# Agent attention with a mixture-of-experts tail: the list scheduler's prices for transfers and its table of urgencies

## The chip, the cores and the metric

The kernel runs on one core of a Trainium2 chip. The core has five engines with an instruction queue each: TensorE (PE in the profile, its weight loads PEld), VectorE (DVE), ScalarE (ACT), GpSimd (POOL) and SyncE (SP), which issues nearly all transfers. The metric is the device time of one execution in microseconds, as the median of several runs.

## The reference

Four batches of 12608 tokens with 128 channels, 49 agents per batch. What is computed:

```python
def _attn_ref(q, k, v, agents):
    a2k = sm(agents, k)            # softmax over the 12608 tokens, scale 1/sqrt(128)
    agent_v = a2k @ v
    q2a = sm(q, agents)            # softmax over the 49 agents
    return q2a @ agent_v

def _moe_ref(x, w_gate, w1, w2, capacity):      # x is the attention's output, capacity 128
    scores = np.einsum('bsd,d->bs', x, w_gate)
    out = x.copy()
    for b in range(B):
        top_idx = np.argpartition(-scores[b], capacity)[:capacity]
        xe = x[b, top_idx]
        ye = np.maximum(xe @ w1, 0.0) @ w2
        g = 1.0 / (1.0 + np.exp(-scores[b, top_idx]))
        out[b, top_idx] = x[b, top_idx] + g[:, None] * ye
```

So each batch has a pass over k and v that gives 49 rows, a pass over q that applies them to every token, the choice of the 128 tokens with the highest gate score, and an expert network for those alone.

## The kernel before, in words

A batch is cut into seven chunks: six of 15 columns of 128 tokens and one of 9. A name such as S_2_3_0 holds the batch, the chunk and the part. The steps of a batch are these.

- "k": SP loads a chunk of k (tile xT, about 0.96 MB), TensorE multiplies it with the agents in two halves (S), VectorE transposes each half into a buffer sk and takes a maximum (mx).
- "kmax": the maxima are brought together over the partitions (mT, mB) into mb. "exp": POOL subtracts mb, ScalarE takes the exponential.
- "v" and "av": SP loads a chunk of v, TensorE adds its products with sk into one PSUM bank (av), 15 for a chunk. "fin": the sum is scaled and split into two half-precision parts, the weights ws (pw, pp).
- "q" and "qe": the same scores for a chunk of q (sq), the maximum qm, POOL's subtraction, ScalarE's exponential, and a half-precision pair f. For batch 0 alone (EARLY) VectorE also sums sq, takes a reciprocal, and POOL multiplies, so that its outputs need no division later.
- "turn": TensorE transposes f (fT, 15 for a chunk), and ScalarE copies the result to ft; for the first part of a chunk of batch 0 VectorE does. "gate": small products pg with the gate's weights.
- "rank": VectorE makes the scores from pg (r, reduce, reciprocal, product), finds the top eight of each partition (MAX8), TensorE spreads them (all0, all1), VectorE and ScalarE compare (ge, ga), and pc gives the token numbers idx.
- "out" and "fill": two products per column give the output (po), which VectorE, or ScalarE with POOL, writes into a tile og, and SP stores it.
- "expert": POOL gathers the chosen rows of q (xq), once for batches 0 to 2 together and once for batch 3, TensorE turns them (qT) and runs the network (sc, eT, xT, xe, ph, py), and POOL scatters the results to the outputs. A batch's scatter waits for all of that batch's stores.

Tiles come from rings. The ring "in" has six buffers for the xT and v tiles and for the og tiles of batches 1 to 3; the ring "sk" has nine, for sk, for the ft tiles of batch 3 and for the two held weight tiles w1_held and w2_held.

The order of all this is not written out. A recorder keeps every instruction with its dependences, and a list scheduler (the function place) then runs through a model of the engines: whenever an engine of the model is free, it takes from the ready instructions whose ring has a buffer the one with the lowest number in the table RANKS, less a bonus STICK if it is of the kind that the engine did last. An instruction of TensorE that waits for another engine counts as ready only after a further SLACK. Durations come from the method price; a transfer ends in the model at a time that place computes from its size, one transfer after another. The instructions are then issued in that order, and on the chip each engine keeps it. All of them carry the line of that loop in the profile.

Of the kernel before, what the change touches and what calls it, by code (L numbers as in the profile page):

```python
# [45 lines left out]
TURN = ('VA', 'AA', 'AA', 'AA')  # L46
FILL = [(0, c) for c in range(7)]
AV_STEP = 5
SLACK = 220.4
STICK = 75.55  # L50
N_OG = 2
SOLO = 5
FT_LAST = 'sk'
# [196 lines left out]

AFTER = {"S": 90.0, "av": 200.0, "po": 100.0, "fT": 20.0}
WARM, COLD, HOLD = 3413.0, 0.45, 4500.0


def lag(a, b):
# [22 lines left out]
def place(rec, urgency, slack=0.0, stick=0.0):  # L278
# [8 lines left out]
    rank = [(urgency(op.tag), op.seq) for op in ops]  # L287
# [12 lines left out]
    line, clock = 0.0, Clock()  # L300
    while len(order) < len(ops) or ends:
# [3 lines left out]
        while ends and ends[0][0] <= now + 1e-6:  # L305
            op = ops[heapq.heappop(ends)[1]]
# [11 lines left out]
        for e, waiting in queue.items():  # L318
            if free[e] > now + 1e-6:
                continue  # L320
            best = None
            for op in waiting:
                if ready[op.seq] > now + 1e-6:
                    continue
                key = rank[op.seq]
                if op.kind == last[e]:
                    key = (key[0] - stick, key[1])
                if best is not None and key >= best[0]:
                    continue
                need = takes[op.seq]  # L330
                if all(room[r] >= need.count(r) for r in need):
                    best = (key, op)
            if best is None:
                continue
            op = best[1]
            waiting.remove(op)
            order.append(op)
            for r in takes[op.seq]:
                room[r] -= 1
            op.start = max(now, free["POOL"]) if op.two else now  # L340
            cost = op.cost
            if e == "PE":
                if last[e] != op.kind:
                    op.start += AFTER.get(last[e], 50.0)
                cost = clock.cost(op, op.start)
            last[e] = op.kind
            free[e] = op.end = op.start + cost
            if op.kind == "dma_start":
                line = max(line, op.start + 1600.0) + op.size / 395.0
                op.end = line + 300.0  # L350
            elif op.size:
                op.end += 2400.0
            heapq.heappush(ends, (op.end, op.seq))
            heapq.heappush(times, op.end)
            heapq.heappush(times, free[e])
# [1 line left out]


RANKS = {
    "setup": 11.4,  # L360
# [5 lines left out]
    },  # L366
    "kmax": {0: -51.2, 1: -208.6, 2: -323.3, 3: 293.3},
    "exp": {
# [4 lines left out]
    },  # L373
# [5 lines left out]
    },  # L379
# [5 lines left out]
    },  # L385
    "fin": {0: -226.7, 1: -86.9, 2: 1.9, 3: -68.6},
# [5 lines left out]
    },  # L392
# [5 lines left out]
    },  # L398
    "turn": {
# [4 lines left out]
    },  # L404
    "gate": {
# [4 lines left out]
    },  # L410
    "rank": {0: -408.8, 1: 398.3, 2: -2.6, 3: 436.6},
    "weights": {0: 46.5},
    "fill": {
        0: {0: -36.2, 1: -253.5, 2: -41.6, 3: 10.2, 4: -42.1, 5: 308.5, 6: 354.6},
    },
    "out": {
# [3 lines left out]
    },  # L420
    "expert": {2: 449.8, 3: -591.5},
}


def urgency(tag):

    r = RANKS.get(tag[0], 0.0)
    for x in tag[1:]:
        r = r.get(x, 0.0) if isinstance(r, dict) else r
    return r  # L430
# [55 lines left out]
def agent_attention_moe(ctx, tc, qT, kT, va, agT, wgb, w1, w2, consts, qs, outs, capacity):  # L486
# [716 lines left out]
    if fast:  # L1203
        for group in GROUP:
            with rec.at("expert", group[-1]):
                run(expert(group, 0, [taken[x] for x in group]))
    order = place(rec, urgency, SLACK, STICK)
    rec.on = False
# [84 lines left out]
```

## Time and profile before

| | before |
|---|---|
| runs | 326.95, 328.5, 329.0 us (median 328.5) |
| profiled execution | 326.07 us, span 324.3 us |
| instructions | 8565 |
| TensorE busy | 279.5 us (86%) |
| VectorE, ScalarE, POOL busy | 222.2, 168.9, 179.7 us |
| mean granted TensorE clock | 0.954 |
| transfers | 106.70 MB, mean 329 GB/s |
| chain that ended last | PE 51%, DMA 19%, DVE 13%, ACT 10%, issue 4% |

The span is the time from the first to the last instruction; the profiled execution's own time is 1.8 us longer. Busy times add up instructions of an engine, overlapping ones once. The granted clock is a share of 2.4 GHz.

### The profile page before, as it was taken

What the parts mean: (1) busy time and instruction counts of PE and PEld (TensorE: products, weight loads), DVE (VectorE), ACT (ScalarE), POOL (GpSimd) and SP (SyncE); (2) the same over time, 40 slices, a digit from 0 to 9 for tenths busy, and PEclk for the clock granted to TensorE, in tenths of its full rate; (3) what the DMA queues carried; (4) which work ended last, traced back from release to release, by engine and by line L of the source; (5) the groups of instructions that cost most, each with busy time, mean ns of one, the idle gap of its engine ahead of it and who ended that gap; (6) DMA issues with size and microseconds to landing.
All of it is one profiled execution on the core that took longest, in us unless ns stands there. A gap on an engine that the chain in (4) does not pass through costs nothing.

```text
span 324.3 us, 8565 instructions
## 1 busy us (share of the span) xinstructions
PE 279.5 (86%) x3524; PEld 185.5 (57%) x3524; DVE 222.2 (69%) x507; ACT 168.9 (52%) x306; POOL 179.7 (55%) x152
## 2 busy tenths in 40 slices
PE   2868699977999999999779988999968895989793
PEld 0213233536554565667556545666968784989493
DVE  0889958973689667767794988774445673889630
ACT  1223438955245578628670086779428583575320
POOL 1357339997553399531950064998706473278232
PEclk9989979997999999999999999999959996699998
DMA  7999999997999999999999998996974275399630
GB/s 293 422 415 386 338 398 344 336 330 271 372 421 413 418 418 406 409 402 408 387 377 349 345 379 342 352 376 233 367 293 181 111 318 206 123 391 405 263 131 30
DMA packets 18204, 106.70 MB, mean 329 GB/s; under 512 B 2032, under 2 KB 3440, under 8 KB 18160
## 3 DMA queue, kind: packets, MB, share of 16 engines
q1 hardware_dynamic: 17472, 105.07, 83.3%
q8 instruction: 30, 0.49, 0.6%
q0 software_dynamic: 256, 0.52, 0.5%
q10 hardware_dynamic: 432, 0.50, 0.4%
q14 instruction: 14, 0.11, 0.1%
HBM read 79.87 MB, written 26.21 MB: 327 GB/s over the span
## 4 chain that ended last, share of the span: by engine, by line
PE 51%; DMA 19%; DVE 13%; ACT 10%; issue 4%; POOL 2%; ACTq 0%; POOLq 0%; DVEq 0%
PE S L1214 18%; PE av L1214 12%; DMA v<-va 8%; PE po L1214 8%; ACT ga L1214 5%; PE fT L1214 5%; DMA xT<-qT 4%; DMA xq<-q,idx 4%; DVE ge L1214 4%; DMA cst<-consts 2%; PE py L1214 2%; PE all L1214 2%; DVE qm L1214 2%; PE ph L1214 2%; ACT ft L1214 2%
## 5 line engine op out<-in xcount | busy, mean ns | idle before, releaser
L1214 PE MATMUL S<-xT,ag_sb 128*32 128x480 f32 (+1 forms) x896 | 103.6, 575 | 17.6 <-DMA ag_sb<-agT 6.1
L1214 POOL TENSOR_TENSOR sq<-sq,qm 128x735 f32<-128x735 f32 (+1 forms) x35 | 47.8, 1368 | 57.1 <-DVE qm L1214 54.1
L1214 PEld LDWEIGHTS <-ft 98*128 98x128 f16 x1188 | 59.7, 99 | 19.7 <-issue 18.3
L1214 POOL TENSOR_TENSOR f<-sq,f 128x735 f16<-128x735 f32 (+1 forms) x28 | 41.2, 1475 | 38.1 <-ACT f L1214 33.2
L1214 PE MATMUL av<-v,sk 128*64 128x129 f32 x792 | 54.5, 287 | 5.4 <-DMA v<-va 5.1
L1214 PE MATMUL po<-ws,ft 98*128 98x128 f16 x792 | 56.0, 224 | 1.0 <-DVE og L1214 0.3
L1214 ACT COPY ft<-fT 98x896 f16<-98x896 f16 (+2 forms) x49 | 43.3, 892 | 25.2 <-PE fT L1214 22.9
L1214 PEld LDWEIGHTS S<-xT,ag_sb 128*32 128x32 f32 x896 | 23.7, 111 | 56.7 <-issue 22.9
L1214 PEld LDWEIGHTS av<-v,sk 128*64 128x64 f32 x792 | 48.3, 143 | 11.8 <-DMA v<-va 6.5
L1214 POOL TENSOR_TENSOR og<-og,r 128x512 f32<-128x512 f32 (+1 forms) x39 | 36.0, 943 | 28.9 <-ACT og L1214 28.0
L1214 POOL TENSOR_TENSOR sk<-sk,mb 128x735 f32<-128x735 f32 (+1 forms) x28 | 47.0, 1711 | 4.4 <-DVE mb L1214 4.3
L1214 DVE STREAM_TRANSPOSE sq<-S 128x480 f32<-128x480 f32 (+1 forms) x56 | 35.5, 644 | 13.2 <-PE S L1214 10.5
L1214 DVE STREAM_TRANSPOSE sk<-S 128x480 f32<-128x480 f32 (+1 forms) x56 | 34.3, 633 | 9.9 <-PE av L1214 9.6
L1214 PEld LDWEIGHTS <-f 128*98 128x98 f16 x396 | 25.9, 127 | 24.3 <-issue 17.8
L1214 DVE TENSOR_REDUCE mx<-S 128x1 f32<-128x480 f32 (+1 forms) x56 | 33.2, 614 | 7.8 <-PE S L1214 7.1
L1214 ACT ACTIVATE sq<-sq,lift 128x735 f32<-128x735 f32 (+1 forms) x28 | 24.8, 887 | 23.6 <-POOL sq L1214 23.6
L1214 PE MATMUL fT<-idh,f 128*98 128x128 f16 x396 | 31.3, 226 | 4.0 <-POOL f L1214 1.9
L1214 DVE SCALAR_TENSOR_TENSOR ge<-all,top,minus 128x512 bf16<-128x512 f32 x32 | 23.9, 746 | 15.7 <-ACT ga L1214 8.7
L1214 DVE TENSOR_REDUCE qm<-sq 128x15 f32<-128x735 f32 (+1 forms) x35 | 30.1, 862 | 2.7 <-ACT sq L1214 2.2
L1214 ACT CAST f<-sq 128x735 f16<-128x735 f32 (+1 forms) x28 | 22.1, 789 | 18.3 <-PE fT L1214 13.6
L1214 DVE TENSOR_TENSOR og<-po,r 128x512 f32<-128x512 f32 (+1 forms) x42 | 26.8, 654 | 6.4 <-PE av L1214 3.3
L1214 ACT ACTIVATE ga<-all,top 128x512 bf16<-128x512 f32 x32 | 22.0, 687 | 11.8 <-DVE ge L1214 10.7
(130 smaller groups left out, 233.9 us busy)
## 6 DMA issues: line engine op xcount, KB each, us to landing
v<-va SPq DMA_DIRECT2D x24, 967.5 KB, 7.1
xT<-qT SPq DMA_DIRECT2D x24, 960.0 KB, 7.1
xT<-kT SPq DMA_DIRECT2D x24, 960.0 KB, 9.3
out<-og SPq DMA_DIRECT2D x24, 960.0 KB, 5.7
v<-va SPq DMA_DIRECT2D x4, 580.5 KB, 5.4
xT<-kT SPq DMA_DIRECT2D x4, 576.0 KB, 8.6
xT<-qT SPq DMA_DIRECT2D x4, 576.0 KB, 5.3
out<-og SPq DMA_DIRECT2D x4, 576.0 KB, 7.0
```

The lines of the kernel that those rows point to most:

```text
L1214: call(*args, **kwargs)
```

## The change

Two prices of place are changed and one is added: a transfer starts 1800 ns after its issue where it was 1600, moves 408 bytes per ns where it was 395, and is known to be complete 1700 ns after its last byte where it was 300. A gather of xq completes 6500 ns after its issue and a scatter 2400 ns, where both were 2400. Under these prices the numbers of the table RANKS, SLACK and STICK were chosen anew. No instruction is added or taken away.

```diff
-SLACK = 220.4
-STICK = 75.55
+SLACK = 320.2
+STICK = 143.58
...
+RATE, GATHER, SCATTER = 408.0, 6500.0, 2400.0
...
             if op.kind == "dma_start":
-                line = max(line, op.start + 1600.0) + op.size / 395.0
-                op.end = line + 300.0
+                line = max(line, op.start + 1800.0) + op.size / RATE
+                op.end = line + 1700.0
             elif op.size:
-                op.end += 2400.0
+                op.end += GATHER if op.label.startswith("xq") else SCATTER
...
     "k": {
-        0: {0: -654, 1: -654, 2: -576.1, 3: -611.8, 4: -589.3, 5: -462.6, 6: -507.5},
+        0: {0: -901, 1: -597.9, 2: -529.2, 3: -621.9, 4: -476.7, 5: -740.5, 6: -614.3},
```

What the table makes of the order is seen in the built programs. The first place is VectorE at the start of the program, behind its constants. Before:

```order
L1214 STREAM_TRANSPOSE sq_0_5_206<-S_0_5_0_208 128x15x32
L1214 STREAM_TRANSPOSE sq_0_5_206<-S_0_5_1_209 128x15x32
L1214 TENSOR_REDUCE qm_0_5_210<-sq_0_5_206 128x15
L1214 STREAM_TRANSPOSE sq_0_3_188<-S_0_3_0_190 128x15x32
L1214 STREAM_TRANSPOSE sq_0_3_188<-S_0_3_1_191 128x15x32
L1214 TENSOR_REDUCE qm_0_3_192<-sq_0_3_188 128x15
L1214 STREAM_TRANSPOSE sq_0_4_197<-S_0_4_0_199 128x15x32
L1214 TENSOR_REDUCE qm_0_5_210<-sq_0_5_206 128x15
L1214 STREAM_TRANSPOSE sq_0_4_197<-S_0_4_1_200 128x15x32
L1214 STREAM_TRANSPOSE sk_0_0_110<-S_0_0_0_112 128x15x32
L1214 TENSOR_REDUCE qm_0_4_201<-sq_0_4_197 128x15
```

And now:

```order
L1215 STREAM_TRANSPOSE sq_2_3_453<-S_2_3_0_455 128x15x32
L1215 STREAM_TRANSPOSE sq_2_3_453<-S_2_3_1_456 128x15x32
L1215 TENSOR_REDUCE qm_2_3_457<-sq_2_3_453 128x15
L1215 TENSOR_REDUCE mx_0_109<-S_0_0_0_112 128x1
L1215 STREAM_TRANSPOSE sk_0_0_110<-S_0_0_0_112 128x15x32
L1215 TENSOR_REDUCE mx_0_109<-S_0_0_1_113 128x1
L1215 STREAM_TRANSPOSE sk_0_0_110<-S_0_0_1_113 128x15x32
L1215 STREAM_TRANSPOSE sk_0_5_130<-S_0_5_0_132 128x15x32
L1215 TENSOR_REDUCE mx_0_109<-S_0_5_0_132 128x1
L1215 TENSOR_REDUCE mx_0_109<-S_0_5_1_133 128x1
L1215 STREAM_TRANSPOSE sk_0_5_130<-S_0_5_1_133 128x15x32
```

Before, three q chunks of batch 0 stood first, with their second reduce; now one q chunk of batch 2 stands first and the k chunks of batch 0 follow at once.

The second place is TensorE at the end of the gate products of batch 3, where the first gathered rows are turned (qT_0_0). Before:

```order
L1214 LDWEIGHTS ft_3_6_619
L1214 MATMUL pg_3_567<-ws_3_556,ft_3_6_619 128x3
L1214 MATMUL qT_0_0_782<-idf_96,xq_0_0_778 128x128 x3
L1214 MATMUL all0_3_627<-idf_96,top_3_623 128x128 x4
L1214 LDWEIGHTS ft_3_1_574
L1214 MATMUL po_3_1_0_716<-ws_3_556,ft_3_1_574 128x128
```

And now, with the place to which qT_0_0 has gone, after 86 more products po, in the second piece:

```order
L1215 LDWEIGHTS ft_3_1_574
L1215 MATMUL pg_3_567<-ws_3_556,ft_3_1_574 128x3
L1215 MATMUL all0_3_627<-idf_96,top_3_623 128x128 x4
L1215 LDWEIGHTS ft_3_4_601
L1215 MATMUL po_3_4_0_731<-ws_3_556,ft_3_4_601 128x128
```

```order
L1215 LDWEIGHTS ft_3_2_583
L1215 MATMUL po_3_2_0_721<-ws_3_556,ft_3_2_583 128x128
L1215 MATMUL qT_0_0_782<-idf_96,xq_0_0_778 128x128 x3
L1215 LDWEIGHTS ft_3_2_583
L1215 MATMUL po_3_2_4_722<-ws_3_556,ft_3_2_583 128x128
```

The row that needs the gather has gone back, and all0_3 follows pg directly.

The third place is SP's queue at the last loads, those of the weights and of v of batch 3, with stores (out) between them. Before:

```order
L1214 DMA w1_held_640<-w1 128x896
L1214 DMA v_3_5_548<-va 128x1935
L1214 DMA out0<-og_0_6_672 128x1152
L1214 DMA xT_3_1_569<-qT 128x1920
L1214 DMA w2_held_641<-w2 128x7x128
L1214 DMA v_3_2_545<-va 128x1935
L1214 DMA out1<-og_1_5_701 128x1920
L1214 DMA v_3_3_546<-va 128x1935
L1214 DMA out1<-og_1_6_706 128x1152
L1214 DMA v_3_6_549<-va 128x1161
L1214 DMA v_3_4_547<-va 128x1935
```

And now:

```order
L1215 DMA v_3_0_542<-va 128x1935
L1215 DMA w1_held_640<-w1 128x896
L1215 DMA w2_held_641<-w2 128x7x128
L1215 DMA v_3_2_545<-va 128x1935
L1215 DMA out1<-og_1_0_676 128x1920
L1215 DMA v_3_3_546<-va 128x1935
L1215 DMA out1<-og_1_3_691 128x1920
L1215 DMA v_3_6_549<-va 128x1161
L1215 DMA out0<-og_0_5_667 128x1920
L1215 DMA v_3_4_547<-va 128x1935
```

The two weight tiles now stand together, directly ahead of four chunks of v, and a store of batch 0 stands ahead of the last one.

## Rows read from the trace of the kernel before

**Rows 1.** The view of busy time by stretch, with nine stretches that begin and end where TensorE stood. Columns: stretch and its length in us, then busy us (and instructions) of each engine, the granted clock, the busy share of the 16 DMA engines, and GB/s.

```profile
0.00:49.00 49.00, 34.52 (x302) 11.56 (x303) 35.08 (x69) 15.49 (x24) 19.71 (x25) 0.93 0.96 375
49.00:75.40 26.40, 21.73 (x241) 10.19 (x238) 21.06 (x36) 20.42 (x29) 26.11 (x18) 1.00 0.95 343
75.40:100.00 24.60, 24.52 (x297) 15.33 (x297) 16.27 (x33) 8.76 (x12) 13.24 (x10) 0.93 0.91 358
100.00:147.60 47.60, 46.46 (x635) 27.92 (x635) 35.73 (x69) 29.20 (x44) 28.80 (x21) 1.00 1.01 411
147.60:187.20 39.60, 35.88 (x514) 24.05 (x510) 30.19 (x82) 17.19 (x39) 15.71 (x11) 1.00 0.98 369
187.20:230.40 43.20, 39.91 (x513) 27.06 (x511) 32.25 (x77) 33.42 (x59) 33.33 (x27) 1.00 0.91 334
230.40:259.20 28.80, 24.09 (x380) 22.03 (x377) 12.77 (x34) 14.87 (x30) 11.80 (x11) 0.88 0.57 229
259.20:274.60 15.40, 11.14 (x222) 10.25 (x222) 8.15 (x31) 9.73 (x23) 8.20 (x10) 0.87 0.71 284
274.60:324.30 49.70, 41.30 (x438) 37.08 (x438) 30.68 (x83) 19.86 (x51) 22.84 (x25) 0.91 0.55 219
```

**Rows 2.** The same view with stretches of 10 us: the first two, and one of the tail.

```profile
0.00:10.00 10.00, 3.87 (x20) 0.93 (x24) 1.39 (x10) 1.76 (x5) 0.83 (x10) 1.00 0.83 318
10.00:20.00 10.00, 7.42 (x64) 1.69 (x56) 9.93 (x17) 2.96 (x4) 4.32 (x3) 1.00 1.02 416
...
270.00:280.00 10.00, 6.41 (x63) 5.95 (x61) 5.90 (x16) 2.79 (x7) 1.82 (x2) 0.52 0.40 156
```

**Rows 3.** The timeline of VectorE in the head: start, duration of the merged piece, instruction, tiles, and how many were merged.

```profile
9.53 1.24 DVE L1214 STREAM_TRANSPOSE sq<-S 128x480 f32<-128x480 f32 x2
...
21.20 1.68 DVE L1214 TENSOR_REDUCE qm<-sq 128x15 f32<-128x735 f32 x2
...
31.22 2.15 DVE L1214 TENSOR_REDUCE mx<-S 128x1 f32<-128x480 f32 x4
...
34.25 0.65 DVE L1214 COPY ft<-fT 98x1024 f16<-98x1024 f16 x1
...
35.21 0.80 DVE L1214 STREAM_TRANSPOSE sq<-S 128x288 f32<-128x288 f32 x2
...
67.79 0.66 DVE L1214 STREAM_TRANSPOSE sk<-S 128x480 f32<-128x480 f32 x1
```

**Rows 4.** The timeline of TensorE at the end of the head; in brackets the idle time before and what ended it.

```profile
75.42 4.74 PE L1214 MATMUL av<-v,sk 128*64 128x129 f32 x50 [1.85 <-DMA v<-va]
```

**Rows 5.** Pieces of TensorE's work at full clock: four from the chain of waits (start, duration, line and how many rows) and one from the timeline, which has the short chunk. A product of 32-bit numbers has two rows in the trace, so that a half chunk of S is 8 rows and 15 products av are 30.

```profile
28.50 0.97 PE fT L1214 x15
...
63.16 1.91 PE av L1214 x30
...
71.87 1.18 PE L1214 MATMUL S<-xT,ag_sb 128*32 128x288 f32 x16
...
84.26 0.94 PE S L1214 x8
...
265.02 1.69 PE po L1214 x30
```

**Rows 6.** The page's part on transfers by line (size each, median us from issue to landing), and the shortest, median and longest landing of the v tiles.

```profile
v<-va SPq DMA_DIRECT2D x24, 967.5 KB, 7.1
xT<-kT SPq DMA_DIRECT2D x24, 960.0 KB, 9.3
out<-og SPq DMA_DIRECT2D x24, 960.0 KB, 5.7
...
DMA to landing us min/median/max: 4.6/7.0/12.0
```

**Rows 7.** The chain of waits: three transfers on it (start, time to landing).

```profile
227.32 10.45 DMA v<-va
...
267.67 6.84 DMA xq<-q,idx
...
297.31 5.76 DMA xq<-q,idx
```

**Rows 8.** The timeline around 237 us, of SP's queue (issues) and of TensorE.

```profile
224.28 0.39 SPq L1214 DMA_DIRECT2D w_held<-w  x1
...
237.81 3.70 PE L1214 MATMUL av<-v,sk 128*64 128x129 f32 x30 [2.63 <-DMA v<-va]
```

**Rows 9.** The timeline around the first gather, of TensorE and of VectorE.

```profile
267.55 2.96 PE L1214 MATMUL pg<-ws,ft 98*128 98x3 f16 x99
...
274.56 0.47 PE L1214 MATMUL qT<-idf,xq 128*128 128x128 f32 x1 [3.59 <-DMA xq<-q,idx]
...
276.53 4.80 PE L1214 MATMUL po<-ws,ft 98*128 98x128 f16 x46
...
272.33 0.27 DVE L1214 MAX8 top<-scs 128x8 f32<-128x99 f32 x1
```

**Rows 10.** The timeline of TensorE at the second gather.

```profile
303.12 0.33 PE L1214 MATMUL qT<-idf,xq 128*128 128x128 f32 x1 [1.92 <-DMA xq<-q,idx]
```

**Rows 11.** What SP's queue waited for, one line each of the stretches 75 to 150 and 150 to 245: us in total, times, longest.

```profile
SPq L1214 <- DVE og L1214: 10.5, 4, 4.2
...
SPq L1214 <- DVE og L1214: 11.4, 4, 4.7
```

More of the change, by code (lines that the diff above doesn't have):

```diff
@@ L359 @@
 RANKS = {
-    "setup": 11.4,
+    "setup": 78.2,
     "k": {
[4 rows of a table removed]
[4 rows of a table added]
     },
-    "kmax": {0: -51.2, 1: -208.6, 2: -323.3, 3: 293.3},
+    "kmax": {0: -378.6, 1: 259.7, 2: -278.6, 3: -446.7},
     "exp": {
[4 rows of a table removed]
[4 rows of a table added]
     },
     "v": {
[4 rows of a table removed]
[4 rows of a table added]
     },
     "av": {
[4 rows of a table removed]
[4 rows of a table added]
     },
-    "fin": {0: -226.7, 1: -86.9, 2: 1.9, 3: -68.6},
+    "fin": {0: -540.4, 1: -165.9, 2: -784.5, 3: -55.5},
     "q": {
[4 rows of a table removed]
[4 rows of a table added]
     },
     "qe": {
[4 rows of a table removed]
[4 rows of a table added]
     },
     "turn": {
[4 rows of a table removed]
[4 rows of a table added]
     },
     "gate": {
[4 rows of a table removed]
-    },
-    "rank": {0: -408.8, 1: 398.3, 2: -2.6, 3: 436.6},
-    "weights": {0: 46.5},
[4 rows of a table added]
+    },
+    "rank": {0: -965.3, 1: -130.5, 2: -13.3, 3: 297.1},
+    "weights": {0: 280.2},
     "fill": {
-        0: {0: -36.2, 1: -253.5, 2: -41.6, 3: 10.2, 4: -42.1, 5: 308.5, 6: 354.6},
+        0: {0: -139.8, 1: -759.5, 2: -179.3, 3: 664.2, 4: 218.6, 5: 414.7, 6: 3.1},
     },
     "out": {
[3 rows of a table removed]
[3 rows of a table added]
     },
-    "expert": {2: 449.8, 3: -591.5},
+    "expert": {2: 372.4, 3: -17.8},
 }
```

68 rows, old and new, of the table RANKS are left out of this document.

## The prediction

> **What bounds the kernel now.** I first cut the span at the places where TensorE stands and read the busy time of each stretch [rows 1]. TensorE works 279.5 of 324.3 us, so some 45 us are to be had, and they lie unevenly: 14.5 idle up to 49.0, 4.7 up to 75.4, then only 8.2 in the 155 us up to 230.4 (26.40-21.73 and so on, from the rows), 4.7 up to 259.2, 4.3 up to 274.6 and 8.4 to the end. The middle is TensorE's own work; an order cannot shorten it. What an order can move is the head, the place near 237 and the tail. All TensorE instructions are the same in both kernels; only their places differ.
>
> In the head three queues press at once. The transfers run at 416 GB/s [rows 2]. VectorE begins at 9.5 us, when a constant has landed, and then works without a gap: it must empty every score tile [rows 3]. And TensorE ends the head with a wait for a v tile, at 75.4 [rows 4].
>
> **Head, the VectorE side.** I price TensorE's work by its steps [rows 5]: half a score chunk 0.94 us (0.59 for the short chunk), 15 turns 0.97, 15 a@v products (30 rows) 1.91. Ahead of the wait at 75.4 stand, counted in the old order, 38 long and 8 short halves, 138 turns and 15 products: 35.7+4.7+8.9+1.9, with two small steps of 0.4 some 52 us. In the new order the same sum is reached after 36 long and 6 short halves, 92 turns and 70 products (33.8+3.5+5.9+8.9+0.8 = 53). I compare VectorE's work up to there, because its queue must be through that far before TensorE is.
> Old: 40 long and 8 short transposes, 18 qm reduces, 24 mx reduces, 4 copies of turned tiles: with 0.62, 0.40, 0.84, 0.54 and 0.65 us each [rows 3] that is 24.8+3.2+15.1+13.0+2.6 = 58.7. New: 36, 6, 12, 24, 2: 22.3+2.4+10.1+13.0+1.3 = 49.1. So 9.6 us of VectorE work leave the head: batch 0 is the one whose q chunks need a second reduce and a copy by VectorE, and three of them stood first. The old floor is 9.5+58.7 = 68.2; the trace has that point at 68.5 (67.79+0.66) [rows 3]. The new floor is 58.6.
>
> **Head, the transfer side.** Bytes issued up to that place: 25.7 MB old, 25.5 MB new (counted in SP's order). 3.2 MB come in the first 10 us, the rest at 416 GB/s [rows 2]: 10+22.3/0.416 = 63.6 us. So the transfers are the new floor, 5 us above VectorE's. The old kernel ended 6.9 above its higher floor (75.4-68.5), because its loads were issued late: from the freeing of a buffer to the need for the tile that takes it, TensorE has 5 to 8.6 us of work for rows 11 to 35 of SP's old order and 6 to 11 in the new (v tiles that are loaded far ahead left out). A load takes 7.1 to 9.3 us in the median [rows 6]. I put the new kernel 4.4 above its floor, at 68: **7.4 us** gained there.
> It is not all kept. When TensorE has done 126 us of work, counted in the same way (batch 1's last a@v), 55.7 MB must have come: 10+52.5/0.416 = 136 us, plus a landing; TensorE alone would be there at 68+126-53 = 141. The margin is 5 us less a landing of some 3 behind the last byte, and the rates of [rows 1] from 49.0 on are 343, 358, 411, 369 GB/s, all under 416. I keep **5.5** (0 to 9; 0 is rival one).
>
> Three tiles have a short lead in the new order, 6.2 us each (v_0_1, one k chunk and the first v of batch 3), against 7.0 in the median of v and 12.0 at most [rows 6]: **-2** (0 to -4).
>
> **Near 237.** The v chunk v_3_3 took 10.45 us to land [rows 7]; TensorE stood 2.63, and after it ran at the lower of its two levels, 1.2 GHz: 30 a@v rows took 3.70 for 1.91 [rows 5, 8], and the stretch has 0.88 [rows 1]. 2.6 and some 2.3 are lost. SP had stood behind the second weight tile, w2_held, until 224.28 [rows 8]; that one needs a score buffer which the last products before it free. In the new order both weights stand directly ahead of v_3_2, v_3_3 and v_3_4, so the same wait is on SP; behind it TensorE has 14 us of work before it wants v_3_3 (12.8 before), 8.6 before v_3_2 (9.9) and 10 between the store out0_5 and v_3_4. With 7.0 us to land all are in time; with 10.45 v_3_2 is 2 us late. I take **+3.5** of the 4.9 (+4.9 to -5, if two chunks wait).
>
> **The first gather.** POOL starts it at 267.67 and it lands 6.84 later [rows 7]; TensorE, whose next row is qT_0_0, stands 3.59 [rows 9] and then runs mostly at 1.2 GHz, 0.52 granted in this stretch [rows 2]: 46 rows of po take 4.80 [rows 9]; at the pace of 30 in 1.69 [rows 5] they take 2.6. In the new order qT_0_0 comes some 7 us of work later (86 po at 1.69/30 and two spreads all of about 1 us) [rows 5]: the gather is hidden. But now all0_3 follows the last pg directly, and it needs VectorE's r, reduce, reciprocal, product and MAX8: from 270.5, when pg ends, to 272.6 [rows 9], 2.1 us, which lay under the gather before. So what goes is 3.6-2.1, **+1.5**, and the slow clock I leave in, since a gap remains. If the clock holds it is +4; if VectorE is busy when pg ends, -1.
>
> **The second gather** is 5.76 us long [rows 7] and leaves a wait of 1.92 [rows 10]. TensorE's work between pc_3, which gives its index, and qT_3 grows from 8.4 to 10.7 us: **+1.9** (0 to 1.9).
>
> **The last stores** are now out0_3 and out3_1, and the scatters of batch 0 and 3 wait for them. po_3_1_0 ends some 9 us of work before the last py; 0.7 to evict and 5.7 to land [rows 6]: covered by 2 us. **0** (to -2).
>
> Sum: 5.5-2+3.5+1.5+1.9 = 10.4. The profiled execution took 326.07 us (span 324.3), so 315.7; it is 2.4 below the median of the three runs, 328.5, from which the sum gives 318.1. I predict **318**.
>
> **Rivals.** *One: the head gives nothing.* If transfers run from the head to 187 at the mean of the four rates in [rows 1], 377 GB/s, 55.7 MB are there at 10+52.5/0.377 = 149, and the old order had 126 us of TensorE work done at the same 149 (75.4-52 = 23.4 behind, as the idle time after the head is small). Against it: in that stretch TensorE was the bound, so the rate is what was asked for. For it: 358 GB/s at a share of 0.91. Time 318+5.5 = 323.5. Chance 0.18.
> *Two: loads land soon, so leads are idle.* If the 4.6 us at the short end of [rows 6] were usual, neither the longer leads nor the three short ones matter: 318+5.5-2 = 321.5. The medians of 7.0 to 9.3 speak against it. Chance 0.05. The Trainium skill's page DMA: Bandwidth & Descriptors (Anatomy of one DMA) fits one transfer as 2.0 us and its bytes at 436 GB/s; for a chunk of 967 KB that is an estimate of 4.3 us. By that rule this rival holds; the trace does not agree, with 7.1 and 9.3 where several are in flight.
> *Three, slower: stores block the loads.* SP issues in order, and four stores of batch 0 stand among the loads of the stretch in which the transfers are the floor. SP waited for such a store four times in 75 to 150, up to 4.2 us, and up to 4.7 later [rows 11]. One load in flight covers 2.3 of it; 2.2 are left, and a wait of that size costs 2.3 more by the clock [rows 8]. Three such are 13.5: 331.5. It decides once a store waits longer than what is queued ahead of it. The old order had the same waits under TensorE's work. Chance 0.08.
> *Four: the change does nothing that counts.* The prices reach only the order; if the new order's idle time lies at other places in the same amount, the time is that of before, 327 to 328. For it: the middle is full, and TensorE's total is fixed. Against: the head's VectorE work is less whatever else happens. Chance 0.14.
>
> **Chances.** My forecast, 0.55, with its own range of 311 to 325. A difference under 1%, 3.3 us, cannot be told from none. Faster than 325.2: nearly all of 0.55, most of rivals one and two (0.16): 0.70. Slower than 331.8: half of rival three, a little of four and the unforeseen: 0.09. Between: 0.21. The range of 8 in 10 is **311 to 329**: it takes in rivals one, two and four and leaves out three and the best ends of all terms together.
>
> **What would show it.** In the profile after: TensorE's idle time before 75 us falls from 19 to some 12, with av of batch 0 begun before 55 us (63.16 before [rows 5]); transfers at 0.95 and more up to 140; no wait of PE for xq; a wait of some 2 us at all<-idf,top behind pg; at most 1 us for v after 180. I am wrong if TensorE comes to wait for xT or v in the middle, between 75 and 230 us, if SP waits long for og before 150, or if the slow clock covers more of the tail than now.

## The result and the profile after

| | before | after |
|---|---|---|
| runs | 326.95, 328.5, 329.0, 325.57 us (median 327.73) | 317.42, 313.12, 312.15, 312.07 us (median 312.63) |
| ratio to before | | 0.9525, 95% interval 0.9454 to 0.9596 |
| profile shown: time, span | 326.07, 324.3 us | 311.66, 309.9 us |
| TensorE busy | 279.5 us | 274.7 us |
| mean granted clock | 0.954 | 0.971 |
| transfers, mean | 329 GB/s | 344 GB/s |

The change is 15.1 us faster by the medians; 10.4 was forecast. In a later comparison of five rounds it was 312.24 for 326.14 us by the medians and 0.9699 (0.9594 to 0.9804) by the ratio, some 10 us; the kernel before scattered from 320.3 to 330.0 us there. Medians here are of all runs, ratios of the fast ones alone, those within 1.5% of the quickest of their kernel in the same comparison. The gain is thus clear, and its size lies between 10 and 15 us. The profile shown is that of the later comparison, since the first profiled execution, 317.42 us, was the longest of all runs of the change.

The view of busy time by stretch, with the stretches of [rows 1]; the last ends with the span.

```profile
0.00:49.00 49.00, 37.63 (x330) 12.63 (x332) 37.94 (x72) 19.22 (x27) 23.38 (x26) 0.97 0.98 397
49.00:75.40 26.40, 24.85 (x319) 14.66 (x323) 19.59 (x34) 16.10 (x22) 20.17 (x14) 1.00 1.01 414
75.40:100.00 24.60, 23.69 (x312) 14.65 (x304) 18.89 (x43) 14.85 (x23) 18.18 (x14) 1.00 1.02 417
100.00:147.60 47.60, 43.88 (x592) 26.89 (x589) 37.98 (x74) 25.81 (x42) 27.95 (x20) 1.00 0.99 398
147.60:187.20 39.60, 38.32 (x527) 22.28 (x529) 31.40 (x73) 22.97 (x39) 21.66 (x16) 1.00 0.96 373
187.20:230.40 43.20, 38.96 (x576) 31.58 (x568) 27.23 (x76) 30.90 (x59) 30.42 (x24) 0.96 0.79 307
230.40:259.20 28.80, 26.14 (x469) 24.64 (x467) 19.76 (x56) 19.20 (x44) 16.57 (x19) 0.97 0.72 290
259.20:274.60 15.40, 12.16 (x151) 11.57 (x152) 12.41 (x31) 9.88 (x25) 7.44 (x8) 0.83 0.50 200
...
274.60:309.90 35.30, 29.09 (x273) 25.11 (x269) 18.22 (x56) 11.18 (x28) 14.19 (x16) 0.94 0.54 217
```

To compare such rows I take TensorE's work at full pace: busy time less the share of the clock that was not granted (37.63 - 0.03 x 49 = 36.2 in the first row). Up to 100 us that is 84.7 after and 75.6 before: **9.1 us** gained. From 100 to 230.4 it is 119.4 for 122.2: 2.8 given back. From 230.4 to 259.2 it is 25.3 for 20.6: **4.6** gained. From 259.2 to the end TensorE falls 14.2 behind its work for 19.1: **4.9** gained. These add up to 15.8; the spans differ by 14.4. The two sums of all work differ by 1.4, since the clock is rounded and the ends of products are modelled; so far the terms are good.

They compare one execution of each kernel, and both kernels scatter. In the head there are more to compare, since several of the kernels below keep one of the two orders there. Up to 100 us the same sum is 81.2 to 84.7 in six executions of the new order and 74.3 in a second one of the old (the kernel in which w2_held is moved): 6 to 10 us gained. Of the 9.1, 5.4 are less idle time and 3.7 a higher clock, and the clock up to 49 us differs between executions of one order: 0.93 to 1.00 in those six.

What TensorE waited for, in the new kernel (us in total, times, longest):

```profile
PE S L1215 <- DMA ag_sb<-agT: 6.1, 1, 6.1
PE all L1215 <- DVE top L1215: 2.2, 1, 2.2
PE S L1215 <- DMA xT<-kT: 2.2, 3, 1.2
...
PE all L1215 <- DVE ge L1215: 2.0, 1, 2.0
...
PE all L1215 <- ACT ga L1215: 1.9, 1, 1.9
PE S L1215 <- DMA xT<-qT: 1.8, 3, 1.1
...
PE av L1215 <- DMA v<-va: 0.9, 1, 0.9
```

And in the kernel before:

```profile
PE qT L1214 <- DMA xq<-q,idx: 5.5, 2, 3.6
PE av L1214 <- DMA v<-va: 5.1, 3, 2.6
PE S L1214 <- DMA xT<-qT: 4.7, 4, 2.7
PE S L1214 <- DMA xT<-kT: 3.5, 3, 2.6
PE all L1214 <- ACT ga L1214: 2.3, 2, 1.4
```

Waits for loads fell from 13.3 to 4.9 us and those for the gathers from 5.5 to none. Three waits of some 2 us stand ahead of the spreads all that were not there, or were shorter. The loads themselves land no sooner; the page's part on transfers now, beside [rows 6]:

```profile
v<-va SPq DMA_DIRECT2D x24, 967.5 KB, 7.5
xT<-qT SPq DMA_DIRECT2D x24, 960.0 KB, 8.8
xT<-kT SPq DMA_DIRECT2D x24, 960.0 KB, 9.4
```

### The profile page after: what moved, and what is told of

It is laid out like the page before. It is cut to its first block, busy times and chain, and to the rows that moved or that the text cites. A ratio compares the mean times of both kernels' runs of the same rounds, so it can differ in the third digit from the quotient of the medians.

```text
span 315.5 us, 8552 instructions
## 1 busy us (share of the span) xinstructions
PE 281.1 (89%) x3524; PEld 190.8 (60%) x3524; DVE 223.1 (71%) x507; ACT 170.8 (54%) x306; POOL 179.9 (57%) x152
## 4 chain that ended last, share of the span: by engine, by line
PE 43%; DMA 26%; DVE 13%; ACT 10%; issue 4%; POOL 1%; ACTq 0%; POOLq 0%; SPq 0%; DVEq 0%
PE S L1215 12%; PE po L1215 10%; DMA xT<-kT 9%; PE av L1215 8%; DMA xT<-qT 6%; ACT ga L1215 5%; DMA v<-va 5%; DVE ge L1215 4%; PE fT L1215 4%; DMA wg_sb<-wgb 3%; DMA out<-og 3%; PE py L1215 2%; PE all L1215 2%; PE ph L1215 2%; PE pg L1215 2%
## 5 line engine op out<-in xcount | busy, mean ns | idle before, releaser
L1215 PE MATMUL S<-xT,ag_sb 128*32 128x480 f32 (+1 forms) x896 | 100.2, 563 | 13.5 <-DMA ag_sb<-agT 6.2
L1215 PEld LDWEIGHTS <-ft 98*128 98x128 f16 x1188 | 65.8, 104 | 18.7 <-issue 15.8
L1215 PE MATMUL po<-ws,ft 98*128 98x128 f16 x792 | 61.9, 238 | 3.0 <-DVE og L1215 1.8
L1215 PE MATMUL av<-v,sk 128*64 128x129 f32 x792 | 53.3, 282 | 1.9 <-DMA v<-va 1.2
L1215 PEld LDWEIGHTS av<-v,sk 128*64 128x64 f32 x792 | 46.4, 139 | 9.3 <-DMA v<-va 3.0
L1215 DVE STREAM_TRANSPOSE sk<-S 128x480 f32<-128x480 f32 (+1 forms) x56 | 35.0, 636 | 11.8 <-PE S L1215 6.6
L1215 PEld LDWEIGHTS <-f 128*98 128x98 f16 x396 | 26.3, 129 | 15.0 <-issue 10.4
L1215 ACT ACTIVATE ga<-all,top 128x512 bf16<-128x512 f32 x32 | 22.0, 686 | 19.1 <-DVE ge L1215 19.0
L1215 ACT ACTIVATE sk<-sk 128x735 f32<-128x735 f32 (+1 forms) x28 | 22.1, 795 | 13.9 <-POOL sk L1215 13.9
```

The source lines that it names most:

```text
L1215: call(*args, **kwargs)
```

## Experiments: which floor held the head

**The change once more.**

> The changed kernel once more, for a second profile of it. All theories: about 312 us, some 15 below the kernel before, as in its other runs. What is open is where it lies. The forecast's own split says: TensorE has done 5.5 us more work at 100 us (busy time less half of the time at 1.2 GHz), 3.5 more came between 230 and 260, 3.4 more at the two gathers. A rival split: the head gives all of what the floor moved, over 7 us, and the rest is the clock, that is fewer stretches at 1.2 GHz in the tail.

312.24 us. By the stretches above the rival split is the nearer one: the head gives more than was kept, and the tail more than the gathers.

**Two tables crossed.** On the kernel before, four numbers of the change:

```diff
 "q":
-        0: {0: -215.7, 1: -288.2, 2: -256.2, 3: -913.1, 4: -687, 5: -941.7, 6: 12.2},
+        0: {0: -215.7, 1: -288.2, 2: -256.2, 3: -125.3, 4: 36.2, 5: -401.6, 6: 12.2},
...
-        2: {0: 57.3, 1: 32.9, 2: 196.2, 3: 157.2, 4: -138, 5: -143.1, 6: -504.8},
+        2: {0: 57.3, 1: 32.9, 2: 196.2, 3: -1010.3, 4: -138, 5: -143.1, 6: -504.8},
```

> The kernel before with its old prices; only the table's q numbers of chunks 3, 4 and 5 of batch 0 and chunk 3 of batch 2 are those of the change. So one q chunk of batch 2 stands first on VectorE and the k chunks of batch 0 follow, as in the change, but the loads are still issued late: 3.6 to 7 us of TensorE's work from a buffer's freeing to the need for the tile up to place 30, 5 to 5.5 for three tiles near place 50. Read: how far TensorE is behind its own work at the last product of batch 0's av and at pw_0 (23.5 us in the kernel before, 16.2 in the change). VectorE theory (the reductions and copies of batch 0's q chunks are what filled the head): 16 to 17. Load theory (the short leads are): 22 to 24. Both in parts: 19 to 21. The whole time tells little, since batch 0's ranking comes 25 us later in this order.

On the changed kernel, the old values of the same four numbers:

> The opposite: the changed kernel with its new prices, but with the old numbers for the q chunks 3, 4 and 5 of batch 0 and chunk 3 of batch 2. Two q chunks of batch 0 stand first on VectorE again, as before the change, and the loads are issued early: 9 to 12 us of TensorE's work ahead up to place 25, 7 to 9.5 at most later ones, 3.1 and 3.8 for two k chunks near place 37. VectorE's work to the place 33 is up to 5 us more than in the change. Read: TensorE's distance behind its own work at pw_0. VectorE theory: 21 to 24, as before the change. Load theory: 16 to 17, as in the change. Both in parts: 18 to 21.

385.83 and 375.97 us, and pw_0, the first product on batch 0's finished sum, at 106.48 and 109.70 us: 34.0 and 33.5 us behind the work ahead of it, far outside what either theory had. The edits did not isolate anything. One row of TensorE in the first of them shows why (start, duration, tiles; in brackets the idle time and what ended it):

```profile
56.61 1.84 PE L1214 MATMUL fT<-idh,f 128*98 128x128 f16 x15 [4.85 <-POOL f L1214]
```

The list scheduler put turns where TensorE then waited 4.85 us for POOL (1.2 at most in the kernel before), and SP stood up to 14.6 us in one wait for TensorE. A number of this table means something only beside all the others. For the rest I kept an order and changed what it costs.

**A seventh buffer for loads, and lighter VectorE work.** Both on the kernel before, in its own order on every engine.

```diff
-N_FT = 14
+N_FT = 13
...
-    inp = rec.pool(ctx.enter_context(tc.tile_pool(name="inp", bufs=N_IN)), "inp", N_IN)
+    inp = rec.pool(ctx.enter_context(tc.tile_pool(name="inp", bufs=7)), "inp", N_IN)
```

> The kernel before, in its own order on every engine, with a seventh buffer in the ring of the xT, v and og tiles (its room comes from two ft buffers that are never in use). Each load can start one tile earlier, so TensorE has 7 to 11 us of work from a buffer's freeing to the need for the tile in place of 5 to 8.6. VectorE's work is unchanged. Read: the start of pw_0, which stands behind 72.5 us of TensorE's work: 96.04 in the kernel before. Load theory (the head was lost to late loads): 88 to 91. VectorE theory (its floor of 68.2 us was the bound): 94 to 96. Both in parts: 91 to 94. The whole time by the load theory is 8 us or more below the kernel before, as v_3_3 near 237 comes in time too; by the VectorE theory 2 to 5, from that place alone.

```diff
         for op in order:
             for call, args, kwargs in op.calls:
+                if op.engine == "DVE" and op.label.startswith("qm_0_") and "axis" in kwargs:
+                    args = (args[0], args[1][:, :, :1])
+                if op.engine == "ACT" and op.label.startswith("sq_0_") and "scale" in kwargs:
+                    kwargs = dict(kwargs, scale=0.02 * kwargs["scale"])
                 call(*args, **kwargs)
```

> The kernel before, in its own order, with lighter work on VectorE in the head: the 14 reductions of q of batch 0 read 1 of the 49 agents in place of all (so batch 0's maximum and sum are those of one agent, and its exponential is taken of a fiftieth of the score). Some 9 us of VectorE's work leave the head, as many as left it in the change by the prediction's count. Loads are issued by the same rules as before. Read: the start of pw_0, 96.04 in the kernel before. VectorE theory: 87 to 90. Load theory: 94 to 96. Both in parts: 91 to 94.

> Both edits on the kernel before: the seventh buffer and the light reductions of batch 0. If one of the two was the bound and the other idle, the start of pw_0 is where that one alone puts it. If they share the 7 us, as I now think, it is 87 to 89, below either alone; the change, with its other order, has 92.2 and 91.1 there with 76.0 us of TensorE's work ahead, which is 87.6 to 88.7 on the scale of 72.5.

The seventh buffer: 317.49 us for 326.68, ratio 0.9776 (0.9639 to 0.9914). The light reductions: 327.27, ratio 0.9999 (0.9937 to 1.0062). Both: 317.65 us. The timelines of TensorE at pw_0, one row each of the kernel before, of the seventh buffer, of the light reductions, of both, and of the change:

```profile
96.04 0.46 PE L1214 MATMUL pw<-avs,cst 128*98 128x129 f32 x2
```
```profile
90.15 0.46 PE L1214 MATMUL pw<-avs,cst 128*98 128x129 f32 x2
```
```profile
97.47 0.46 PE L1218 MATMUL pw<-avs,cst 128*98 128x129 f32 x2
```
```profile
90.40 0.46 PE L1218 MATMUL pw<-avs,cst 128*98 128x129 f32 x2
```
```profile
91.07 0.46 PE L1215 MATMUL pw<-avs,cst 128*98 128x129 f32 x2 [0.29 <-DVE mb L1215]
```

The buffer alone moves pw_0 by 5.9 us, the lighter VectorE by nothing, and both together no more than the buffer. The change has 3.5 us more of TensorE's work ahead of pw_0, so its 91.07 is 87.6 on the old scale, 8.4 gained. Five other executions of its head have pw_0 at 91.19 to 93.23, so 6.3 to 8.4 are gained; a second one of the old order has it at 96.29. VectorE did lose its work; the stretch from 9.5 to 30 us, before and with the light reductions (third busy column):

```profile
9.50:30.00 20.50, 15.22 (x131) 4.49 (x127) 18.87 (x33) 6.13 (x12) 11.59 (x8) 0.92 1.02 418
```
```profile
9.50:30.00 20.50, 12.03 (x104) 3.51 (x104) 12.94 (x31) 5.62 (x12) 11.47 (x8) 0.92 1.02 415
```

18.87 became 12.94 and TensorE was not a product further (104 rows for 131): the transfers ran at 415 for 418 GB/s, and TensorE waited 3.29 and 2.09 us for k. In the kernel before it had waited for k too, 2.58 us at the first of these places, and for VectorE only once in this stretch, 0.53 us. The row of the kernel before, then the two with the light reductions:

```profile
21.47 3.40 PE L1214 MATMUL S<-xT,ag_sb 128*32 128x480 f32 x16 [2.58 <-DMA xT<-kT]
```
```profile
21.81 1.82 PE L1218 MATMUL S<-xT,ag_sb 128*32 128x480 f32 x16 [3.29 <-DMA xT<-kT]
...
28.03 3.43 PE L1218 MATMUL S<-xT,ag_sb 128*32 128x480 f32 x16 [2.09 <-DMA xT<-kT]
```

The bytes moved by 100 us order the kernels as their work does (GB/s times length, summed over the first three stretches; work as above):

| by 100 us | light | before | seven | after |
|---|---|---|---|---|
| MB moved | 35.8 | 36.2 | 39.1 | 40.6 |
| TensorE's work, us | 73.2 | 75.6 | 81.2 | 84.7 |

4.4 MB more at 415 GB/s are 10.6 us of transfers. The table alone does not say which of the two causes the other; the seventh buffer does, as it changes nothing but when a load can start. That is the head: in the old order a load was issued too late to keep the 16 DMA engines full from 49 us on (343 and 358 GB/s in [rows 1]), and the new order, or a seventh buffer (390 and 416), keeps them full or nearly so. The loads that TensorE stood for from 40 to 100 us had left SP 5.4 to 6.7 us ahead of the need in the profile before, and 8.7 to 11.0 us in the profile of the change.

**A seventh buffer in the changed kernel.** The same edit; its room comes from one of two xT tiles of the expert and two of four rate tiles.

> The changed kernel in its own order with a seventh buffer in the same ring (its room comes from buffers of the expert's and the rate's tiles that are never in use at once). If loads still bound anything in the changed kernel, the waits of TensorE for xT and v, some 6 us in its second profile, go: 4 to 7 us faster than the changed kernel, about 306 to 308. If the transfers' rate is the bound there, since they already run at 415 GB/s from 20 to 100 us, the buffer gives 0 to 2: about 311.

313.24 us, ratio 0.9651 (0.9535 to 0.9766): no difference from the change. Its stretches:

```profile
49.00:75.40 26.40, 25.19 (x331) 15.36 (x332) 20.65 (x34) 16.26 (x22) 20.54 (x15) 1.00 1.01 414
75.40:100.00 24.60, 23.61 (x315) 14.70 (x308) 18.58 (x43) 15.01 (x24) 17.85 (x14) 1.00 1.02 416
100.00:147.60 47.60, 44.68 (x590) 27.33 (x583) 38.84 (x74) 25.50 (x42) 28.73 (x21) 0.98 1.01 412
```

The same rates up to 100 us, the same work. What was worth 7 us (by the ratio) to 9 us (by the medians) in the old order is worth nothing in the new one: the transfers are its floor there. The Trainium skill, page Perfetto Trace Analysis, section Roofline, holds that a lone core is bounded by its 16 DMA engines at about 435 GB/s; the rows agree with a bound of that kind, at 412 to 417.

## Experiments: the place near 237, the gathers, the gaps that are left

**w2_held issued late,** on the kernel before. The function moved takes the named instructions of an engine out of the order and puts them directly ahead of the first one of another name; out2's first store stands directly behind v_3_4.

```diff
+MOVES = [("SP", ["w2_held"], "out2")]
...
     order = place(rec, urgency, SLACK, STICK)
+    order = moved(order)
```

> The kernel before with one instruction moved: SP issues w2_held behind v_3_4 in place of ahead of v_3_2. SP then no longer stands behind w2_held until 224.28 with v_3_2, v_3_3 and v_3_4 queued behind it. By the prediction's step on the place near 237: the wait of 2.63 us for v goes, and with it the stretch at 1.2 GHz behind it: 3 to 5 us faster than the kernel before, 322 to 323. Rival: v_3_3 is late because the transfers ahead of it are (its own landing took 10.45 us); then the wait stays over 1.5 us and the time within 2 us of before.

324.89 us for 327.01, ratio 0.9965 (0.9917 to 1.0013): not told from no change. In its profile the wait for v behind 230 us is gone and the stretch keeps its clock, 1.00 where [rows 1] have 0.88:

```profile
187.20:230.40 43.20, 36.72 (x455) 25.31 (x451) 28.50 (x62) 30.75 (x51) 30.47 (x23) 0.96 0.86 313
230.40:259.20 28.80, 26.79 (x450) 23.32 (x442) 16.44 (x47) 17.36 (x38) 14.67 (x15) 1.00 0.70 263
```

But this execution had lost 4.9 us of work in the stretch ahead of it, by waits for loads that were issued before the moved one. And the loads left SP no sooner: v_3_2 left behind the same a@v product as w2_held and v_3_2 had (within 0.5 us of its end in both kernels), and v_3_3 7.8 us ahead of the need for it, as before (7.9). So SP had not stood for w2_held alone; with it gone it stands at the same place. What differs is v_3_3's landing, 7.42 us for 10.45 before and 10.51 in the run with the light reductions, which has w2_held in its old place. Whether that is the 0.46 MB of w2_held ahead of it or TensorE's own waits, which spread the loads, is not shown. The seventh buffer did not remove the wait either:

```profile
229.21 3.18 PE L1214 MATMUL av<-v,sk 128*64 128x129 f32 x29 [2.53 <-DMA v<-va]
```

What the change did there can be read in its SP queue: both weights are out by 205 us, where w2_held stood until 224.28 before [rows 8].

```profile
197.08 7.96 SPq L1215 DMA_DIRECT2D w_held<-w  x2
```

**The gather at its old price.**

```diff
-RATE, GATHER, SCATTER = 408.0, 6500.0, 2400.0
+RATE, GATHER, SCATTER = 408.0, 2400.0, 2400.0
```

> The changed kernel with the gather priced 2400 ns in place of 6500, all other prices and the table as changed. Only the tail's order moves: qT_0_0 stands again between the last pg and all0_3, and qT_3 has 8.8 us of TensorE's work behind pc_3 in place of 10.7. By the prediction's steps both waits come back, 3.6 for 2.1 at the first gather and 1.9 at the second: 3.4 us slower than the changed kernel. Rival: the wait for the top eight behind pg is as long as the gather's, so nothing changes at the first and the kernel is 0 to 2 us slower. Second rival: the clock falls behind the longer wait and costs as much again, 5 to 7 us slower.

315.15 us (313.69 to 316.91) beside 312.24 (310.79 to 315.0) on the same chip: 2.9 slower. Both waits are back:

```profile
261.64 0.48 PE L1215 MATMUL qT<-idf,xq 128*128 128x128 f32 x1 [2.73 <-DMA xq<-q,idx]
...
290.44 0.33 PE L1215 MATMUL qT<-idf,xq 128*128 128x128 f32 x1 [2.08 <-DMA xq<-q,idx]
```

In the changed kernel the first stands as a wait for the top eight, and the second is gone (rows of its timeline):

```profile
260.71 2.04 PE L1215 MATMUL all<-idf,top 128*128 128x128 f32 x8 [2.24 <-DVE top L1215]
...
289.35 0.27 PE L1215 MATMUL qT<-idf,xq 128*128 128x128 f32 x1
```

This one price, with the table unchanged, accounts for a fifth of the gain by the medians, and up to three tenths if the gain is 10 us.

**Work moved into the gaps.** Two kernels move products of the changed kernel ahead of the spreads that wait, with the same function: the first with the first list, the second with the other.

```diff
+MOVES = [("PE", ["po_3_4_0", "po_3_4_4", "po_3_4_8", "po_3_4_12"], "all0_3")]
...
+MOVES = [("PE", ["po_3_4_0", "po_3_4_4", "po_3_4_8", "po_3_4_12"], "all0_3"),
+         ("PE", ["po_0_2_8", "fT_1_1_0"], "all1_0"),
+         ("PE", ["po_1_0_4", "po_1_3_8", "po_1_3_12"], "all1_1")]
```

> The changed kernel with one edit of TensorE's order: the four groups of po_3_4 (30 products, some 1.8 us) stand ahead of all0_3 in place of behind it, so that TensorE has work while VectorE makes the top eight of batch 3. The wait of 2.24 us behind the last pg goes to under 0.7. By the prediction's step on the first gather this wait is on the path: 1.5 to 2 us faster, and up to 3.4 more if the stretch of 6.8 us at 1.2 GHz that lies there in the changed kernel goes with it: 307 to 310.5. Rival: the path there runs through the ranking of batch 3 (all0, ge, ga, pc, the second gather), which now starts later by nothing, so TensorE's gap only moves to qT_3 and the time stays within 1 us of 312.

> The edit of the tail and two more like it: po_0_2_8 and the first turn of f_1_1 stand ahead of all1_0 (wait of 2.02 us for VectorE's ge at 145), and three groups of po, 1.7 us, ahead of all1_1 (wait of 1.87 us for ScalarE's ga at 198). If these two new waits are what took back part of the head's gain, 2 to 3 us go beside the tail's, and up to 1.7 for the clock behind the second: 3 to 5 us faster than the tail's edit alone, 303 to 307. If the transfers bound TensorE from 100 to 200 us (they run at 398 and 373 GB/s there), the time goes into waits for xT and v right after, and it is within 1 us of the tail's edit alone.

319.82 and 320.14 us: by the medians 7 to 8 slower than the change (whose kernel before was 326.14 us, where it is 327.01 here), which neither theory had. By the ratios to the kernel before it is less clear: 0.9715 (0.9652 to 0.9777), not told from the change's 0.9699, and 0.9864 (0.9802 to 0.9925), slower. The profiles decide it: from the last gate product to the end of the span the change takes 51.4 us, these two 58.0 and 57.6, with the same work. The tail of the first of them, on TensorE:

```profile
265.55 3.36 PE L1236 MATMUL po<-ws,ft 98*128 98x128 f16 x30 [2.92 <-DVE og L1236]
268.70 2.02 PE L1236 MATMUL all<-idf,top 128*128 128x128 f32 x8
272.98 1.03 PE L1236 MATMUL po<-ws,ft 98*128 98x128 f16 x8 [2.25 <-DVE og L1236]
```

The four banks for po were full of po_3_3, which stands ahead of pg. It can only be emptied with the rate r, and VectorE makes r from the last pg, ahead of the top eight. So the moved products waited longer than all0_3 had, all0_3 behind them too, and the stretch from 259.2 to 274.6 was granted a clock of 0.59. In the middle the second kernel cut the wait at all1_0 from 2.02 to 0.93, and 1.24 came back at the next a@v (the row below); the wait of 1.87 at all1_1 went, and 0.80 and 0.98 came at the products moved ahead of it. At 230.4 us it had done 203.7 us of work, the change 204.1.

```profile
150.95 1.32 PE L1236 MATMUL av<-v,sk 128*64 128x129 f32 x19 [1.24 <-ACT sk L1236]
```

**The gate products first.** The last kernel heeds this: po_3_3 itself goes behind pg.

```diff
     order = place(rec, urgency, SLACK, STICK)
+    late = [op for op in order if op.engine == "PE" and op.label.startswith("po_3_3_")]
+    order = [op for op in order if op not in late]
+    last = max(n for n, op in enumerate(order) if op.engine == "PE" and op.label.startswith("pg_3"))
+    order[last + 1:last + 1] = late
```

> The changed kernel with one edit of TensorE's order that heeds what the two runs before showed: the four banks for po are full of po_3_3, whose results need the rate r, and r comes only from the last pg. So here the gate products are not followed by more po; po_3_3 itself (30 products, 1.85 us) goes from ahead of the last pc of batch 2, of the last turns and of pg to behind the last pg. The last pc, the turns, pg and VectorE's chain to the top eight then begin 1.85 us earlier, and po_3_3 fills the time in which TensorE stood. The wait of 2.24 us goes to 0 to 0.7, less up to 0.6 that pg waits for ScalarE's copies of the last turns: 1.2 to 2 us faster than the changed kernel, and up to 3.4 more if the stretch at 1.2 GHz at 257 to 264 goes: 307 to 311, a ratio to the kernel before of 0.955 to 0.965 where the changed kernel had 0.970. Rival: VectorE and ScalarE must then empty po_3_3 and po_3_4 one behind the other, so TensorE waits as long for a bank: within 1 us of the changed kernel.

313.99 us (310.64 to 314.69), ratio 0.9667 (0.9607 to 0.9728): within 2 us of the change, no gain that can be told. The wait is gone as expected:

```profile
256.38 2.54 PE L1219 MATMUL pg<-ws,ft 98*128 98x3 f16 x90
259.08 0.39 PE L1219 MATMUL pg<-ws,ft 98*128 98x3 f16 x9 [0.16 <-issue]
259.33 3.36 PE L1219 MATMUL po<-ws,ft 98*128 98x128 f16 x30
262.49 2.02 PE L1219 MATMUL all<-idf,top 128*128 128x128 f32 x8
```

po_3_3 took 3.36 us in place of 1.85, and three small waits, 0.54 together, came around pg: 2.24 went and about 2 came. Two stretches of this kernel, during pg and behind it:

```profile
256.00:259.00 3.00, 2.92 (x97) 2.72 (x95) 0.20 (x3) 1.52 (x2) 2.67 (x3) 1.00 0.79 323
259.30:262.50 3.20, 3.20 (x38) 3.20 (x35) 2.74 (x10) 0.85 (x2) 0.39 (x1) 0.50 0.77 293
```

TensorE was busy for 2.92 of 3.00 us with gate products, three columns each, and then without a pause; the granted clock fell to 0.50, 1.2 GHz, all the same. So the slow stretch needs no such wait, and to fill the wait won nothing. When it begins differs: in the change the clock had fallen ahead of the last gate product (0.76 granted from 257.0 to 258.4, the wait from 258.47 on), in the second kernel with moved work it stood at 1.00 until 260, two us behind the last one. It comes around the end of the gate products in every tail here; that they cause it is not shown.

## Why the prediction was right, and where it was not

The time lies in the range, 311 to 329, and in the forecast's own, 311 to 325; the gain was 15.1 us for 10.4, and some 10 to 14 in the later comparison. The signs came too: TensorE stood 12.9 us up to 75.4 (some 12 were said), batch 0's a@v began at 48.9, and no wait for xq is left. But one of the two reasons given for the head was wrong.

- **Head, the VectorE side: failed.** The prediction took "9.6 us of VectorE work leave the head" as the cause and a VectorE floor of 68.2 us, met by the trace at 68.5, as the bound. With some 6 us of that work gone from 9.5 to 30 us alone, pw_0 came no sooner (97.47 for 96.04 and 96.29), and beside the seventh buffer no sooner either (90.40 for 90.15). So the agreement of 68.2 and 68.5 proved nothing; VectorE, which begins at 9.5 and shows hardly a pause until 40 us, kept pace with the loads and did not set it.
- **Head, the transfer side: right.** "Its loads were issued late" was there as the remainder of 6.9 us over the floor; it was the whole. The seventh buffer alone gave 5.9 of it. The new floor by transfers is also as said: 414 to 417 GB/s from 49 to 100 us, and a seventh buffer adds nothing. The place that the prediction put at 68 us (36 long and 6 short halves, 92 turns, 70 products) is reached at 67.3 in the profile shown, at 67.3 to 69.1 in six executions of that head; the 4.4 us over the floor that went into the 68 had no row behind them, so that it came out so near is luck in part.
- **What is kept of the head: undersized.** 5.5 was kept and 2 taken off for three short leads; 9.1 are there at 100 us (6 to 10 with the other executions) and 6.3 at 230. The short leads cost nothing that shows. Where 2.8 were given back, two spreads, all1_0 and all1_1, wait 2.02 and 1.87 us for VectorE and ScalarE; they stand 6.2 and 7.0 us of work behind their first halves (7.1 and 25.0 in the old order), and no term of the sum had them. That they are what gave it back is not shown: in the second kernel with moved work these waits were shorter or gone, and no more was done by 230.4 us.
- **Near 237: right in its size,** 4.6 for 3.5, and that in part by luck. The wait for v is 0.95 us now. That w2_held was its cause is not shown: to move it alone was worth 2.7 us at most. And the execution with the light reductions, w2_held in its old place, did 23.9 us of work in this stretch where the one of [rows 1] did 20.6; so 3.3 of the 4.6 differ between executions of one order there.
- **The gathers: right,** 2.9 for 3.4 together. The swap of 3.59 for 2.1 at the first came out as 2.24; at the old price in the new table the wait there was 2.73, so only 0.5 of the 2.9 lies in it and 2.08 in the second. The slow clock was left in, rightly, though the reason given ("since a gap remains") does not hold: with the gap filled it fell all the same.
- **The tail beyond the gathers:** 4.9 for 3.4 in all. The clock takes 4.7 us of the last two stretches, by the rows above, where it took 6.5 by [rows 1]; that is 1.8 which the sum had at nothing.
- **Rivals.** *The head gives nothing* falls by the 9.1 us. *Loads land soon* falls by the medians of 7.5 to 9.4 us and by what one more buffer was worth. The 4.3 us are an estimate by the fit of the Trainium skill (DMA: Bandwidth & Descriptors, Anatomy of one DMA), which that section gives for the path of GpSimd. The loads here leave from SP, several in flight, and the trace does not agree with it. *Stores block the loads*: SP did wait for og, once for 5.7 us before 150 and once for 8.5 after, but no load came over 1.2 us late. *Nothing that counts* falls by the result.

Not tried: the new table with the old prices of transfers, and the old table with the new prices; so how much of the gain is the prices' and how much the table's is open, but for the gather's price.

## What to carry to other kernels

When an engine is busy without a pause beside a queue of transfers, its work is not yet the bound: add a buffer or lighten the engine, in the same order, and see which of the two moves a late milestone. A move of work into a gap must ask which banks are full and what empties them. And a table of priorities cannot be tested by changing a few of its numbers; keep the order and change what it costs.

## What was not expected of the hardware

TensorE's clock fell to 1.2 GHz behind 99 products of three columns although the engine was busy for 2.92 of 3.00 us and did not stand afterwards; the 30 products behind them took 3.36 us in place of 1.85. After the same 99 products in another kernel of this order it stayed at 2.4 GHz for two us of standing. And the same order of instructions lost or kept up to 4.9 us of work in a stretch from one execution to the next, with waits for loads; the kernel before scatters more (320.3 to 330.0 us) than the change (310.8 to 315.0 in the same comparison, 317.42 at most in the first).
